# Weight requests of the opening chained two at a time, and one chunk's attention output transposed by DMA instead of TensorE, in a one-core transformer block

## The chip, the cores and the metric

One NeuronCore of a Trainium2 chip runs the whole kernel. The metric is device microseconds of one execution, without any host work; lower is better. Five engines work side by side and each takes its instructions in program order: TensorE (PE) multiplies and transposes, VectorE (DVE) and ScalarE (ACT) do elementwise work, GpSimd (POOL) and SyncE (SP) mostly issue DMA requests here.

## The reference

A block of 2048 tokens of width D = 576, in bfloat16, conditioned on one vector c:

```
mod = silu(c) @ w_mod                     # split in six rows: sa, ca, ga, sb, cb, gb
h = layernorm(x) * (1 + ca) + sa
x = x + ga * attention(h)                 # 32 heads of 18, wqkv and wo
h = layernorm(x) * (1 + cb) + sb
x = x + gb * (((h @ w_gate) * (h @ w_up)) @ w_down)      # inner width 4608
```

In the attention, token s looks at the eight tokens s, s-2, ..., s-14 (a window of 8, dilation 2); positions before the first token are masked. Weights are 576 x 1728 (wqkv), 576 x 576 (wo), 576 x 4608 (gate and up), 4608 x 576 (down) and 576 x 3456 (w_mod).

## The kernel before

**Stages.** The 2048 tokens are cut into eight chunks of CH = 256, each of two tiles of 128 ("halves" j = 0 and 1). The chunks are worked in five groups for the large matrix products: [0], [1, 2], [3, 4], [5, 6], [7]. Each group has a gate-and-up phase (`gate_up`, L968) and then a down phase (`down`, L1011; `down_last` for the last group). In both, a loop over 36 values of f goes through the inner width 128 columns at a time. Everything before the first gate phase is here called the opening: the modulation vectors, chunk 0 whole up to its second layernorm, and the first parts of chunks 1 and 2. The layernorms and attention of the later chunks run in pieces between the f steps of earlier groups.

**The order of work.** All five engines keep the order in which the program issues instructions. Between the f steps a planner (`timed`, L899, and `among` for the down phases) places pieces. A piece is a tuple of its cost on PE, its cost on DVE, the marks that it needs, the mark that it gives, a wait until that mark counts, and the call. The planner runs its own clock in these estimates; a thread (a list of pieces) goes on in order, and a piece is placed when its needs are met. The real dependencies are kept by semaphores; the numbers in a piece only move its place.

**Transfers.** SP issues, in program order on one queue, the input chunks (`load_x` L140 and `load_res` L144: tiles x_t and x_r), the gate and up weights and most transposes by DMA. A gate or up block covers FB = 4 values of f; `load_wgu` (L149) brings it by two requests of 512 KB (L158), one for gate and one for up, into a tile wgu. Three such tiles are in rotation (`wgup`), so blocks 0 to 2 of group 0 are loaded in the opening (L1213-1214); block 3 is put into the unused end of the tile hh (`wgu_home[3]`, last part of the program), blocks 4 and on are asked for as blocks come free. The 64 rows that 576 has beyond four times 128 come in two requests by `load_wgr` (L162), into wgr. The down weights are loaded by POOL (`load_wd`, L167, issued at L175; some into space named prod_t or hh). Ahead of the weight requests in the opening go the weights of the modulation (wmA, whose space is loaded a second time at L1211 under the name wmB; the records call it wmA both times) and, behind them, x_t and x_r of chunks 3, 1 and 4. `behind(dma, load)` adds a wait: the first request is not issued before the second has landed.

```
    load_wm_tail(wmB, 3, nc.sync)
    nc.sync.dma_start(wmB[:, 0:KF, :], w_mod[0:KF * P, 3 * D:5 * D]...)      # L1211
    load_wgr()
    for g in range(3):
        load_wgu(g)
```

**The attention output.** For a half, DVE multiplies the gathered values vsh by the attention weights (`b_mul`), adds them up (`b_add`) into o_sb (128 tokens x 640, of which the last 64 columns are a memset, L555, or a repetition, L558). The projection with wo needs o_sb transposed, in oT. This is done in one of two ways: `b_o` (L572) has PE transpose ten 128x128 squares (L578) into two PSUM tiles, which ACT copies to oT (L579, L580); `b_od` (L651) has SP issue one DMA transpose of 128x640 for a half (L653). `b_w(i, j)` (L655) then multiplies a half by wo on PE (L659 for the last 64 columns, L661 for the first 512), and DVE scales the result and adds the input, giving x1 of chunk i. The second layernorm follows (`b_ln`, `b_norm`), then a DMA transpose of its output into h2T (`b_td`, L693) and the modulation in place (`b_mod`). The DMA transpose of the first layernorm's output is `a_td` (L420).

Chunk 0 gets its output by another route; chunks 1 and 2 use `b_o`, chunks 3 to 7 `b_od` (`values_of`, L729; `out_of`).

**The first down phase** (group 0, two halves, four matmuls per f: L1021 into acc, L1026 into accr). Around it, chunk 1 ends its attention block (layernorm, h2T) and chunk 2 its values, output transpose, projection, layernorm and h2T; the list of chunk 2's pieces is `first_down` (L1390). In the same loop SP asks for blocks 0, 1 and 2 of group 1's gate weights behind f = 1, 20 and 26 (`asks`, L1038), and POOL for further down weights (`WD_ASKS`).

Of the kernel before, what the change touches and what calls it, by code (L numbers as in the profile page):

```python
# [18 lines left out]
P = 128  # L19
D = 576  # L20
DP = 640
KT = 5
KF = 4
# [13 lines left out]
FB = 4  # L37
# [5 lines left out]
PAIRED = (1, 3, 5, 7)  # L43
# [3 lines left out]
def kernel(  # L47
# [13 lines left out]
    nc = tc.nc  # L61
# [31 lines left out]
    def ps(shape, dt, name):  # L93
        return psp.tile(shape, dt, name=name, tag="bank")

    def js(j):
        return slice(j * P, (j + 1) * P)
# [14 lines left out]
    wgr = wts.tile([P, FF], BF, name="wgr")  # L112
# [34 lines left out]
    NG = len(GROUPS)  # L147
    NBLK = FT // FB

    def load_wgu(g):  # L150
        if g >= NG * NBLK:
            return
        cs = slice((g % NBLK) * NB, (g % NBLK + 1) * NB)
        wb = wgu_home.pop(g, None)
        if wb is None:
            wb = wgup.tile([P, KF, 2, NB], BF, name="wgu")
        for t, wsrc in enumerate((B_w_gate, B_w_up)):
            r = nc.sync.dma_start(wb[:, :, t, :], wsrc[0:KF * P, cs].rearrange("(k p) n -> p k n", p=P))  # L158
        wgu_blk[g] = wb
        wgu_in[g] = r  # L160

    def load_wgr():  # L162
        for t, wsrc in enumerate((B_w_gate, B_w_up)):
            r = nc.sync.dma_start(wgr[64 * t:64 * (t + 1), :], wsrc[KF * P:D, :])
        return r

    def load_wd(g):  # L167
# [49 lines left out]
    wmB = wmA  # L217
# [257 lines left out]
    def b_ld(i, j):  # L475
        b = bb.setdefault(i, dict(prod={}, vsh={}))
        base = HALO + i * CH + j * P - DIL * (W - 1)
        vsh = vshp.tile([P, W, DH, H], BF, name="vsh")
        vsrc = bass.AP(vd.tensor, vd.offset + base * D, [[D, P], [DIL * D, W], [1, D]])
        b["vsh"][j] = vsh  # L480
        r = nc.gpsimd.dma_start(vsh[:].rearrange("p w d h -> p w (d h)"), vsrc)  # L481
        b.setdefault("ld", r)
        return r
# [62 lines left out]
    def b_mul(i, j, w0, n=2):  # L546
        b = bb[i]
        v = b["vsh"][j][:, w0:w0 + n]
        at = b["attn"][:, j, w0:w0 + n, None, :].to_broadcast([P, n, DH, H])
        nc.vector.tensor_tensor(v, v, at, ALU.mult)  # L550
# [21 lines left out]
    def b_o(i):  # L572
        pA = ps([P, 4, CH], BF, "oT_pA")
        pB = ps([P, 1, CH], BF, "oT_pB")
        for m in range(KT):
            d = pA[:, m, :] if m < 4 else pB[:, 0, :]
            for j in range(ST):
                nc.tensor.transpose(d[:, js(j)], o_sb[:, j, m * P:(m + 1) * P], ident[:])  # L578
        nc.scalar.copy(oT[:, 0:4, :], pA[:])  # L579
        nc.scalar.copy(oT[:, 4, :], pB[:, 0, :])  # L580
# [70 lines left out]
    def b_od(i, tiles=range(ST)):  # L651
        for j in tiles:
            bb[i]["od"] = nc.sync.dma_start_transpose(out=oT[:, :, js(j)], in_=o_sb[:, j, :])  # L653

    def b_w(i, j):  # L655
        pw = ps([P, 512], F32, "pw")
        pwr = ps([P, 64], F32, "pwr")
        for m in range(KT):
            nc.tensor.matmul(pwr[:], lhsT=oT[:, m, js(j)], rhs=wo[:, m, 512:D], start=(m == 0), stop=(m == KT - 1))  # L659
        for m in range(KT):  # L660
            nc.tensor.matmul(pw[:], lhsT=oT[:, m, js(j)], rhs=wo[:, m, 0:512], start=(m == 0), stop=(m == KT - 1))  # L661
        xt = x1p.tile([P, D], BF, name="x1")
        nc.vector.tensor_tensor(xt[:, 512:D], pwr[:], ga_bc[:, 512:D], ALU.mult)
        nc.vector.tensor_tensor(xt[:, 0:512], pw[:], ga_bc[:, 0:512], ALU.mult)
        nc.vector.tensor_tensor(xt[:], xt[:], x_res[i][:, j, :], ALU.add)
        x1.setdefault(i, []).append(xt)
# [62 lines left out]
    def values_of(i, nxt=None):  # L729
        r = []  # L730
        for j in range(ST):
            r += [(0, 0.75, f"a{i}", "-", 0, lambda j=j, w=w: b_mul(i, j, w)) for w in range(0, W, 2)]
            r += [(0, 0.75, "", "-", 0, lambda j=j: b_add(i, j, 0)), (0, 0.75, "", "-", 0, lambda j=j: b_add(i, j, 1)),
                  (0, 1.2, "", f"o{i}{j}", 0, lambda j=j: b_add(i, j, 2))]
            if i in PAIRED[1:]:
                r.append((0, 0, "", f"O{i}" if j == ST - 1 else "-", 11.0 if i == 7 else 14.0, lambda j=j: b_od(i, (j,))))
            if nxt is not None:

                r.append((0, 0, f"v{nxt}", "-", 0, lambda j=j: behind(b_ld(nxt, j), bb[i]["od"]) if (i, j) == (3, 1) else b_ld(nxt, j)))
        return r  # L740
# [270 lines left out]
    def down(gi, hh, bg):  # L1011
        grp = GROUPS[gi]
        nj = ST * len(grp)
        last = FT - FB
        at, late = among(last, 0.25 * nj, bg)
        acc = [ps([P, 512], F32, "acc") for _ in range(nj)]
        accr = ps([P, 2 * ST, 64], F32, "accr")

        def mm_a(f, j):
            wb = wd_blk[gi * NBLK + f // FB]  # L1020
            nc.tensor.matmul(acc[j][:], lhsT=hh[:, f, js(j)], rhs=wb[:, f % FB, 0:512],  # L1021
                             start=(f == 0), stop=(f == FT - 1))

        def mm_r(f, j):
            wb = wd_blk[gi * NBLK + f // FB]
            nc.tensor.matmul(accr[:, j, :], lhsT=hh[:, f, js(j)], rhs=wb[:, f % FB, 512:D],  # L1026
                             start=(f == 0 and j == 0), stop=(f == FT - 1), skip_group_check=True)

        for f in range(last):
            for j in range(nj):  # L1030
                mm_a(f, j)
                mm_r(f, j)
            if f % FB == FB - 1:
                if gi in (1, 2) and f // FB == 1:
                    wd_home[gi * NBLK + 8] = value_space()[:, 0:FB * D].rearrange("p (k d) -> p k d", d=D)
                for k in WD_ASKS[gi].get(f // FB, ()):
                    load_wd(gi * NBLK + k)
            asks = (1, 5 * FB, 6 * FB + 2) if gi == 0 else (1, 4 * FB - 1, 6 * FB + 1)  # L1038
            if f in asks:
                load_wgu((gi + 1) * NBLK + asks.index(f))  # L1040
            for piece in at[f]:
                piece()
        xs = [t for i in grp for t in x1.pop(i)]
        for j in range(nj):
            for f in range(last, FT):
                mm_r(f, j)
        o_ts = [outp.tile([P, D], BF, name="o_t") for _ in range(nj)]
        t_r = outr.tile([P, 2 * ST, 64], BF, name="t_r")
        nc.vector.tensor_tensor(t_r[:, 0:nj, :], accr[:, 0:nj, :],  # L1049
                                gb_bc[:, None, 512:D].to_broadcast([P, nj, 64]), ALU.mult)  # L1050
        for j in range(nj):
            for f in range(last, FT):
                mm_a(f, j)
            nc.vector.tensor_tensor(o_ts[j][:, 0:512], acc[j][:], gb_bc[:, 0:512], ALU.mult)
        for j in range(nj):
            r0 = (grp[0] * ST + j) * P
            nc.vector.tensor_tensor(o_ts[j][:, 0:512], o_ts[j][:, 0:512], xs[j][:, 0:512], ALU.add)
            nc.vector.tensor_tensor(o_ts[j][:, 512:D], t_r[:, j, :], xs[j][:, 512:D], ALU.add)
            nc.sync.dma_start(out_flat[r0:r0 + P, :], o_ts[j][:])
        if gi in (0, 3):  # L1060
            load_wd(gi * NBLK + NBLK + 2)
        return late
# [58 lines left out]
    def behind(dma, load):  # L1121
        tc.add_manual_dep(dma.ins, load.ins.name, SYNC, reason="order of the loads")
# [81 lines left out]
    for dd4 in range(4):  # L1204
        nk = (DH - dd4 + 3) // 4
        wsrc = bass.AP(A_wo.tensor, A_wo.offset + dd4 * D, [[DH * D, H], [4 * D, nk], [1, D]])
# [1 line left out]
    load_x(2)  # L1208
    load_res(0)
    load_wm_tail(wmB, 3, nc.sync)  # L1210
    nc.sync.dma_start(wmB[:, 0:KF, :], w_mod[0:KF * P, 3 * D:5 * D].rearrange("(k p) n -> p k n", p=P))  # L1211
    load_wgr()
    for g in range(3):  # L1213
        load_wgu(g)
    cp, dv = nc.scalar.copy, nc.vector.tensor_copy
    x1c = x_in.pop(1)
    xn1, stat1, rsq1, norm1 = ln_parts(lambda j: x1c[:, j, :], "a", True)
# [170 lines left out]
           4: ([], [])}  # L1388

    def first_down(parts):  # L1390
        o2 = [(0, 0, "o21", "z2", 0.6, nop), (0.55, 0, "z2", "O2", 1.1, lambda: b_o(2)), (1.2, 1.35, "O2", "-", 0, lambda: b_w(2, 0)), (1.2, 1.35, "", "x2", 0.2, lambda: b_w(2, 1)),
              (0, 2.2, "", "s2", 0.7, lambda: b_ln(2)), (0, 1.5, "s2", "n2", 0.2, lambda: b_norm(2)), (0, 0, "n2", "T2", 6.0, lambda: b_td(2)),
              (0, 0, "T2", "M2", 0, lambda: (b_mod(2, (3, 4), False), b_mod(2, (0, 1, 2), True)))]
        return [[(0, 0, "", "-", 0, lambda: ld_prods(0))]] + parts[:-1] + [parts[-1] + o2]
# [16 lines left out]
    for gi, grp in enumerate(GROUPS):  # L1411
        hh_t = hhp.tile([P, FT * 2 * CH], BF, name="hh")
        n = CH * len(grp)
# [46 lines left out]
```

## Time and profile before

| | |
|---|---|
| median of three runs | 538.25 us (537.63 to 538.43) |
| the profiled execution | 538.37 us, of which the span from first to last instruction is 536.5 us |
| PE busy | 530.2 us, 99% of the span, 6365 matmuls and transposes |
| DVE, ACT, POOL busy | 319.3, 251.7 and 70.3 us |
| granted TensorE clock | 1.0 |
| moved by DMA | 114.81 MB, 214 GB/s in the mean |
| SP's queue (q1) | 67.25 MB in 84208 packets, 46.3% of 16 engines' span |
| POOL's queue (q0) | 46.40 MB in 11424 packets, 28.0% |
| 512 KB request of gate weights, issue to landing | median 5.7 us (of up weights 7.2) |

Times in the profile are microseconds from the start of the span, taken in one profiled execution. A line of the timeline gives the start, how long the run of equal instructions took, the engine, the source line and operation, the tiles written and read, shapes and how many. "SPq" and "POOLq" are the queues of these engines: such a line lasts from the first issue to the last of the group, not until the data has landed. In the list of DMA issues the last number is the median from issue to landing. The rows of forty digits show busy shares in tenths, forty equal slices of 13.4 us; PEclk is the granted clock in tenths. The chain of waits follows the work that ended last back to the start and shares the span out by engine.

### The profile page before, as it was taken

What the parts mean: (1) busy time and instruction counts of PE and PEld (TensorE: products, weight loads), DVE (VectorE), ACT (ScalarE), POOL (GpSimd) and SP (SyncE); (2) the same over time, 40 slices, a digit from 0 to 9 for tenths busy, and PEclk for the clock granted to TensorE, in tenths of its full rate; (3) what the DMA queues carried; (4) which work ended last, traced back from release to release, by engine and by line L of the source; (5) the groups of instructions that cost most, each with busy time, mean ns of one, the idle gap of its engine ahead of it and who ended that gap; (6) DMA issues with size and microseconds to landing.
All of it is one profiled execution on the core that took longest, in us unless ns stands there. A gap on an engine that the chain in (4) does not pass through costs nothing.

```text
span 536.5 us, 14991 instructions
## 1 busy us (share of the span) xinstructions
PE 530.2 (99%) x6365; PEld 327.8 (61%) x6365; DVE 319.3 (60%) x748; ACT 251.7 (47%) x629; POOL 70.3 (13%) x109
## 2 busy tenths in 40 slices
PE   8999999999999999999999999999999999999997
PEld 4787888758875444555544454555544454558875
DVE  5898888869777785508467797513527733032212
ACT  4866887605666544103655543104556541006630
POOL 8104013202000110111000011110010101110210
PEclk9999999999999999999999999999999999999999
DMA  9999999899987854969354944963395594659741
GB/s 287 304 272 365 317 267 333 282 256 242 273 203 186 275 107 123 281 184 304 94 170 119 317 125 137 268 185 109 104 320 154 154 301 107 208 140 291 238 124 35
DMA packets 96004, 114.81 MB, mean 214 GB/s; under 512 B 29217, under 2 KB 84722, under 8 KB 95810
## 3 DMA queue, kind: packets, MB, share of 16 engines
q1 hardware_dynamic: 84208, 67.25, 46.3%
q0 software_dynamic: 11424, 46.40, 28.0%
q8 instruction: 50, 0.82, 0.6%
q10 hardware_dynamic: 306, 0.21, 0.1%
q14 instruction: 16, 0.13, 0.1%
HBM read 103.07 MB, written 4.74 MB: 201 GB/s over the span
## 4 chain that ended last, share of the span: by engine, by line
PE 97%; DMA 1%; DVE 0%; SPq 0%; issue 0%; ACT 0%
PE pg L774 29%; PE pu L774 24%; PE acc L1021 20%; PE pq L774 4%; PE pq L442 3%; PE accr L1026 3%; PE acc L1076 3%; PE pv L774 2%; PE pw L774 2%; PE lgT L501 2%; PE pv L465 1%; PE pw L661 1%; DMA wmA<-in_w_mod_dram 1%; PE po L616 1%; PE pwj L638 0%; PE accr L1079 0%
## 5 line engine op out<-in xcount | busy, mean ns | idle before, releaser
L774 PE MATMUL pg<-h2T,wgu 64*128 64x512 bf16 (+1 forms) x1400 | 267.7, 328 | 0.3 <-issue 0.3
L774 PE MATMUL pu<-h2T,wgu 64*128 64x512 bf16 (+1 forms) x1400 | 266.1, 328 | 0.0
L774 PEld LDWEIGHTS <-wgu 64*128 64x128 bf16 x2800 | 140.0, 94 | 90.8 <-issue 0.9
L825 ACT CAST u_sb<-pu 128x512 bf16<-128x512 f32 (+1 forms) x169 | 83.9, 496 | 155.9 <-PE pg L774 150.9
L828 DVE TENSOR_TENSOR hh<-g_sb,u_sb 128x512 bf16<-128x512 bf16 x133 | 56.3, 423 | 109.4 <-ACT g_sb L826 108.5
L1021 PE MATMUL acc<-wd,hh 128*128 128x512 bf16 x344 | 85.7, 380 | 0.0
L1021 PEld LDWEIGHTS <-hh 128*128 128x128 bf16 x504 | 49.0, 98 | 59.7 <-issue 1.5
L826 ACT CAST g_sb<-pg 128x512 bf16<-128x512 f32 (+1 forms) x169 | 84.9, 502 | 0.0
L1026 PE MATMUL accr<-wd,hh 128*128 128x64 bf16 x344 | 62.4, 193 | 0.0
L774 PE MATMUL pu<-h2T,wgr 64*128 64x256 bf16 (+1 forms) x191 | 61.9, 324 | 0.0
L774 PE MATMUL pg<-h2T,wgr 64*128 64x256 bf16 (+1 forms) x191 | 61.9, 324 | 0.0
L1026 PEld LDWEIGHTS <-hh 128*128 128x128 bf16 x504 | 45.8, 98 | 1.2
L175 POOL DMA_DIRECT2D wd<-in_B_w_down_dram x29 | 21.8, 753 | 183.5 <-PE accr L1026 148.2
L550 DVE TENSOR_TENSOR vsh<-vsh,attn 128x1152 bf16<-128x1152 bf16 x56 | 39.5, 750 | 0.0
L489 DVE TENSOR_TENSOR prod_t<-qT,kT 128x1280 bf16<-128x1280 bf16 x36 | 28.2, 819 | 3.5 <-ACT kT L845 2.7
L774 PEld LDWEIGHTS <-wgr 64*128 64x128 bf16 x382 | 19.7, 94 | 15.0 <-issue 2.3
L1021 PE MATMUL acc<-prod_t,hh 128*128 128x512 bf16 x112 | 28.1, 380 | 0.0
L774 PE MATMUL pq<-hT,wqk 64*128 64x256 bf16 (+1 forms) x450 | 26.8, 258 | 0.0
L774 PEld LDWEIGHTS <-wqk 64*128 64x128 bf16 x450 | 21.3, 94 | 5.3
L1049 DVE TENSOR_TENSOR t_r<-accr,gb_bc 128x256 bf16<-128x256 f32 (+1 forms) x4 | 1.5, 378 | 38.2 <-PE accr L1026 38.2
L481 POOL DMA_DIRECT2D vsh<-vd x14 | 12.6, 901 | 86.6 <-DVE o_sb L558 61.8
L1026 PE MATMUL accr<-prod_t,hh 128*128 128x64 bf16 x112 | 21.6, 193 | 0.0
(224 smaller groups left out, 630.4 us busy)
## 6 DMA issues: line engine op xcount, KB each, us to landing
wgu<-in_B_w_gate_dram SPq DMA_DIRECT2D x41, 512.0 KB, 5.7
wgu<-in_B_w_up_dram SPq DMA_DIRECT2D x41, 512.0 KB, 7.2
wd<-in_B_w_down_dram POOLq DMA_DIRECT2D x29, 576.0 KB, 4.9
vsh<-vd POOLq DMA_DIRECT2D x14, 1152.0 KB, 8.5
prod_t<-in_B_w_down_dram POOLq DMA_DIRECT2D x8, 576.0 KB, 6.5
hh<-in_B_w_down_dram POOLq DMA_DIRECT2D x6, 576.0 KB, 6.9
x_t<-in_A_x_dram SPq DMA_DIRECT2D x8, 288.0 KB, 6.0
x_r<-in_A_x_dram SPq DMA_DIRECT2D x8, 288.0 KB, 7.7
```

The source lines that it names most:

```text
L175: return nc.gpsimd.dma_start(wb[:], B_w_down[r0:r0 + FB * P, :].rearrange("(k p) n -> p k n", p=P))
L442: nc.tensor.matmul(pq[:, gi, :], lhsT=wqk[:, kt, m * P:(m + 1) * P], rhs=hT[:, kt, cols], start=(kt == order[0] and not (by_k and gi)), st ...
L481: r = nc.gpsimd.dma_start(vsh[:].rearrange("p w d h -> p w (d h)"), vsrc)
L489: nc.vector.tensor_tensor(prod, aa[i]["qT"][:], aa[i]["kT"][:, :, off:off + CH], ALU.mult)
L550: nc.vector.tensor_tensor(v, v, at, ALU.mult)
L774: return nc.tensor.matmul(out, lhsT=lhs, rhs=rhs, start=first, stop=last, skip_group_check=True)
L825: nc.scalar.copy(u[:, c, :], pu)
L826: nc.scalar.copy(g[:, c, :], pg)
L828: return lambda: nc.vector.tensor_tensor(hh[:, f - c:f + 1, :], g, u, ALU.mult)
L1021: nc.tensor.matmul(acc[j][:], lhsT=hh[:, f, js(j)], rhs=wb[:, f % FB, 0:512], start=(f == 0), stop=(f == FT - 1))
L1026: nc.tensor.matmul(accr[:, j, :], lhsT=hh[:, f, js(j)], rhs=wb[:, f % FB, 512:D], start=(f == 0 and j == 0), stop=(f == FT - 1), skip_grou ...
L1076: nc.tensor.matmul(acc[i][:], lhsT=hh[:, f, js(j)], rhs=wb(f)[:, c0:c1], start=(f == 0), stop=(f == FT - 1))
```

## The change

**The opening.** From the long load of wmB on, seven more requests are noted in a list `longs`: the two of `load_wgr` and gate and up of blocks 0, 1 and 2. With wmB's that makes nine, and each but the first two waits, by `behind`, until the one two places before it has landed; the second wgr request is the first to wait (for wmB), and the gate request of block 0 waits for the first wgr request. After block 2 the list is cleared: later requests do not wait in this way. They stand behind these on SP's queue, though.

**Chunk 2's output.** `b_o(2)` is dropped. `values_of(2)` issues a DMA transpose of a half (`b_od`) as soon as the half is added up, giving the mark D0 or D1, which counts for the planner 8 us later; `b_w(2, 0)` needs D0 and `b_w(2, 1)` D1, separately.

**The asks.** Blocks 1 and 2 of group 1's gate weights are asked for behind f = 26 and 27 of the first down phase, not 20 and 26.

```diff
+    longs = []
+
+    def in_turn(r):
+
+        if longs:
+            longs.append(r)
+            if len(longs) > 2:
+                behind(r, longs[-1 - 2])
+        return r
+
     def load_wgu(g):
...
-            r = nc.sync.dma_start(wb[:, :, t, :], wsrc[0:KF * P, cs].rearrange("(k p) n -> p k n", p=P))
+            r = in_turn(nc.sync.dma_start(wb[:, :, t, :], wsrc[0:KF * P, cs].rearrange("(k p) n -> p k n", p=P)))
...
     def load_wgr():
         for t, wsrc in enumerate((B_w_gate, B_w_up)):
-            r = nc.sync.dma_start(wgr[64 * t:64 * (t + 1), :], wsrc[KF * P:D, :])
+            r = in_turn(nc.sync.dma_start(wgr[64 * t:64 * (t + 1), :], wsrc[KF * P:D, :]))
         return r
...
-            if i in PAIRED[1:]:
+            if i == 2:
+                r.append((0, 0, "", f"D{j}", (8, 8)[j], lambda j=j: b_od(i, (j,))))
+            elif i in PAIRED[1:]:
                 r.append((0, 0, "", f"O{i}" if j == ST - 1 else "-", 11.0 if i == 7 else 14.0, lambda j=j: b_od(i, (j,))))
...
-            asks = (1, 5 * FB, 6 * FB + 2) if gi == 0 else (1, 4 * FB - 1, 6 * FB + 1)
+            asks = (1, 26, 27) if gi == 0 else (1, 4 * FB - 1, 6 * FB + 1)
...
-    nc.sync.dma_start(wmB[:, 0:KF, :], w_mod[0:KF * P, 3 * D:5 * D].rearrange("(k p) n -> p k n", p=P))
+    longs.append(nc.sync.dma_start(wmB[:, 0:KF, :], w_mod[0:KF * P, 3 * D:5 * D].rearrange("(k p) n -> p k n", p=P)))
     load_wgr()
     for g in range(3):
         load_wgu(g)
+    longs.clear()
...
-        o2 = [(0, 0, "o21", "z2", 0.6, nop), (0.55, 0, "z2", "O2", 1.1, lambda: b_o(2)), (1.2, 1.35, "O2", "-", 0, lambda: b_w(2, 0)), (1.2, 1.35, "", "x2", 0.2, lambda: b_w(2, 1)),
+        o2 = [(1.2, 1.35, "D0", "-", 0, lambda: b_w(2, 0)), (1.2, 1.35, "D1", "x2", 0.2, lambda: b_w(2, 1)),
```

## The prediction, made before the result was seen

> **What bounds the kernel now.** I read the page first: busy shares, granted clock, chain.
>
> ```profile
> PE 530.2 (99%) x6365; PEld 327.8 (61%) x6365; DVE 319.3 (60%) x748; ACT 251.7 (47%) x629; POOL 70.3 (13%) x109
> ...
> PEclk9999999999999999999999999999999999999999
> DMA  9999999899987854969354944963395594659741
> ...
> PE 97%; DMA 1%; DVE 0%; SPq 0%; issue 0%; ACT 0%
> ```
>
> PE is busy 99% of the span of 536.5 us at an undiminished clock and is 97% of the chain, so an instruction taken off PE shortens the run by what it occupies there, and a wait added on PE lengthens it in full: no idle time further on can absorb it. Removing waits can bring little, since PE idles only 536.5 - 530.2 = 6.3 us, most of it at the two ends. The DMA row matters too: up to about 107 us (the first eight slices of 13.4 us) the transfer engines are as full as PE, so a transfer delayed there cannot catch up.
>
> Then the timelines of the two places edited. PE in the first down phase, with the transposes that go:
>
> ```profile
> 113.74 0.38 PE L1021 MATMUL acc<-prod_t,hh 128*128 128x512 bf16 x1
> 113.96 0.19 PE L1026 MATMUL accr<-prod_t,hh 128*128 128x64 bf16 x1
> 113.99 0.61 PE L578 MATMUL oT_pA<-shifts,o_sb 128*128 128x128 bf16 x8
> 114.44 0.28 PE L578 MATMUL oT_pB<-shifts,o_sb 128*128 128x128 bf16 x2
> 114.55 0.38 PE L1021 MATMUL acc<-prod_t,hh 128*128 128x512 bf16 x1
> ```
>
> SP's queue in the opening, and for the last weight request its line in the list of issues, whose last number is microseconds to landing:
>
> ```profile
> 22.90 4.89 SPq L158 DMA_DIRECT2D wgu<-in_B_w_gate_dram  x1
> 27.84 3.48 SPq L158 DMA_DIRECT2D wgu<-in_B_w_up_dram  x1
> 31.36 3.58 SPq L158 DMA_DIRECT2D wgu<-in_B_w_gate_dram  x1
> 34.98 1.69 SPq L158 DMA_DIRECT2D wgu<-in_B_w_up_dram  x1
> ...
> 40.73 1.39 SPq L158 DMA_DIRECT2D hh<-in_B_w_up_dram  x1
> ```
> ```profile
> hh<-in_B_w_up_dram SPq DMA_DIRECT2D x1, 512.0 KB, 18.0
> ```
>
> Block 3 of the first gate phase (it lies in hh) is thus complete at 40.73 + 18.0 = 58.7; PE first reads it at 62.07. Last, SP and DVE in the first down phase, where the new transfers go in:
>
> ```profile
> 104.68 2.55 SPq L693 DMA_TRANSPOSE h2T<-xn  x2
> 107.29 0.57 SPq L158 DMA_DIRECT2D wgu<-in_B_w_gate_dram  x1
> ```
> ```profile
> 106.79 0.09 DVE L555 MEMSET o_sb<- 128x32 uint32 x1
> ...
> 112.10 0.09 DVE L555 MEMSET o_sb<- 128x32 uint32 x1
> ```
>
> The memsets end the two halves of chunk 2's attention output: ready at 106.88 and 112.19.
>
> **Part 1, what leaves PE and ACT.** Ten 128x128 transposes go. The matmul ahead of them hands over at 113.99 and the next starts at 114.55: **-0.56 us** on PE. ACT loses the two evictions (L579 1.01 us, L580 0.38 us); it had idled 8.9 us before them, so nothing follows.
>
> **Part 2, the new wait on PE.** In the built order the projection of half 0 (L659, L661) moves from behind f = 27 to behind f = 20; that of half 1 stays behind f = 29. One f takes 0.49 us (50 pairs of matmuls from 101.73 to 113.99), so PE asks for half 0 at 101.73 + 21 x 0.49 = 112.0, that is 5.1 us after the data is ready. Half 1 is asked for where L659 now runs second, 118.22, less 0.56: 117.66, that is 5.5 us after its data. SP stands idle before both and issues at once. How long does a 128x640 transpose take? Rows of the same stage of other groups, with weight loads from POOL in flight: 3.3 (213.07), 4.3 (332.44), 4.4 (449.57), 5.4 (450.87), 5.5 (126.07); in this very stage 6.1 and 9.8 (104.68, 105.98); alone 2.6 (201.24). The bounds are therefore 2.6 and 9.8. I take 4.4, the row nearest in its surroundings (a POOL load issued 0.8 us earlier, as here at 106.12): half 0 lands at 111.4, in time by 0.6; half 1, by 5.4, at 117.7, just in time. **0 us**, with ends 0 and 106.95 + 9.8 - 112.0 = 4.7. What is queued behind a late projection is every later matmul.
>
> Moved with it: two of chunk 2's products (1.4 us) go ahead of chunk 1's layernorm statistics on DVE, and SP now issues half 0, then chunk 1's two h2T transposes (from 104.68 to about 108.2, 1.2 us each), then waits for half 1 at 112.19, and only then asks for weight blocks 1 and 2 of the next gate phase (107.29 to about 113.5). With the 9.8 row h2T lands at 119.2; DVE needs 1.37 us to modulate it and PE reads it from 122.5 - 0.56: covered by 1.4. Block 1 landed 12.8 us after its second issue (107.91): 114.1 + 12.8 = 126.9, against its first use at about 128.4 (four f of 1 us and two value pairs of 1 us after 122.5): covered by 1.5; block 2 (15.9) by 1.7. Cost 0.
>
> **Part 3, the opening.** Seven requests now wait for the one two before them: the second remainder load wgr, and gate and up of blocks 0 to 2. Before, SP simply pushed; the rows of 4.89, 3.48 and 3.58 us show it held back by a full queue, and the landings follow each other every 1.5 us (21.29 + 15.3 = 36.6, 22.21 + 15.9 = 38.1). So 512 KB are 1.5 us of transfer. A 512 KB request into a quiet queue lands after
>
> ```profile
> wgu<-in_B_w_gate_dram SPq DMA_DIRECT2D x1, 512.0 KB, 4.0
> ```
>
> (412.29). With two in flight, two requests move in 4.0 + 0.05 us instead of 3.0: a hole of 1.05 us per pair, the engines idle. Walking it through from the landings that the edit leaves alone (wmB, called wmA in the records, 28.85, first wgr 31.57, second wgr about 35.1): the six weight requests issue at 31.7, 35.2, 36.7, 39.3, 40.8, 43.4 with three holes, 3 x 1.05 = 3.15 us. POOL has little to fill them with before 44 (0.1 MB at 34), so everything behind on SP's queue comes 3.15 us later as long as the engines stay full, which the DMA share of 1.02 to 1.1 between 31 and 63 says they do:
> - block 3: 58.7 + 3.15 = 61.9, against 62.07: just in time.
> - block 4: gate landed at 53.51 + 9.0 = 62.5, up by the 1.5 us spacing at 64.0 (its own landing is not recorded): 67.1, against PE's first use at 66.00: **1.1 us late, paid on PE**.
> - chunk 3's input: issued some 7 us later (43.8), landing about 52 instead of 45.4; DVE wants it at 51.83, and its idle 0.29 and 1.53 us before 58.90 and 61.59 take that up. 0.
> - block 5 lands at 66.8 + 3.15 = 70.0, against 70 + 1.1. 0.
>
> Bounds: nothing, if the hardware's own hold-back already had only about two requests under way; and with 5.0 per request (the up load of the same quiet pair) (5.0 + 0.05 - 3.0) x 3 = 6.2 us, so 6.2 - 2.0 = 4.2 us at block 4. The value of 4.0 is the nearer: it is one request's own duration, the 5.0 includes queueing behind its partner.
>
> The Trainium skill, DMA: Bandwidth & Descriptors, section on the anatomy of one DMA, prices a request at 2.0 us fixed plus its bytes at 436 GB/s. That would be 3.2 us for 512 KB and, as an estimate from that page, 0.25 us per hole and no late block at all; it gives the case without a stall below. This trace does not agree: 4.0 us, and 1.5 us between landings.
>
> **Sum**: -0.56 + 0 + 1.1 = +0.55. The profiled run took 538.37 (span 536.5 and 1.9 around it), 0.1 over the median of 538.25; added to the median: **538.8 us**.
>
> **The rivals.**
> - **No stall at all**: holes add to less than 2.0 us in sum (or the holds change nothing, since SP was held back anyway: the 4.89 us row speaks for it, the 4.0 us row against). 538.25 - 0.56 = 537.7.
> - **The transpose is late on PE**, slower: price is its time to landing less 5.1 us. With 6.1 it is 1.0; from 6.7 on the kernel is slower by over 0.2%, with the 9.8 row +4.1: 542.4. For it: both rows of this very stage are above 6; against it: in the new order half 0 goes first and the weight loads of SP come after.
> - **The opening's holes are larger**, slower: at 5.0 per request +3.7, 541.9. For it: POOL's loads from 44 on take the larger part (0.87 MB against 0.20 MB of SP's queue between 46 and 49), so a request pushed behind 44 moves slowly.
> - **PE gains more than the records show**, faster: if its transposes also cost it the 1.39 us of evictions, 536.3. Against it: PE ran matmuls without a gap straight behind them. The Trainium skill, TensorE: Matmul & The Clock Gate, Part 4 on transposes, has about 275 ns for one in a kernel, which would be 2.75 us for ten, an estimate from that page; the trace has ten in 0.56 us and does not agree.
>
> **How the numbers follow.** Forecast 0.38, of which 0.08 ends above the bound; no stall 0.30; late transpose 0.14; larger holes 0.14; more than the records 0.04. A measurement of this kernel can tell about 0.2% (1.1 us) from no change. Slower by more: 0.08 + 0.14 + 0.14 = 0.36; faster by more: 0.04; within: 0.60. The range begins at 537.3, the case without a stall less 0.4 for the spread of the runs (537.63 to 538.43), and ends at 541.3, which takes in both slow rivals up to about 3.6 us of stall and leaves out their far ends.
>
> **What would show it.** After: no L578 at 114, L659 twice with oT landing by DMA; PE idle before the first of them is the late transpose, by its length. PE idle at 62 (hh) or 66 (wgu) is the opening; the landings of block 3 and 4 should be near 61.9 and 67.1. Landings of the six requests 4 us after issue and a lower DMA rate between 33 and 44 show the holes; an unchanged rate there refutes them and makes 537.7 the result. PE idle in any other place would prove the accounting wrong.

## The result and the profile after

The changed kernel takes 549.94 us (548.60 to 550.72, four runs) against 538.05 (537.63 to 538.43, four runs) for the kernel before on the same chip: a ratio of 1.0222, with a 95% interval of 1.0206 to 1.0238. The forecast was 538.8 with a range up to 541.3. The profiled execution took 550.72, that is 12.35 more than the profiled one of before. One execution of a later run, the one with three requests under way, had a granted clock of 0.56 from end to end (929.20 us) and is in none of the times below. The lines that answer to those shown of before:

```profile
PE 531.5 (97%) x6327; PEld 325.7 (59%) x6355; DVE 319.5 (58%) x748; ACT 251.1 (46%) x627; POOL 70.1 (13%) x109
...
PEclk9999789999999999999999999999999999999999
DMA  9989997979895676697733973994285693758731
...
PE 88%; DMA 6%; DVE 4%; ACT 1%; issue 1%; SPq 0%
```

PE is busy for about as long as before, but its share of the chain has fallen from 97% to 88%. DMA and DVE have taken it. The granted clock, 9 in all forty slices before, falls to 7 and 8 in the fifth and sixth slice (55 to 82 us). So the loss has a place. PE's timeline there (the brackets give the idle time ahead of a line and what ended it):

```profile
56.37 0.27 PE L786 MATMUL pg<-h2T,wgu 64*128 64x256 bf16 x1
59.84 0.28 PE L786 MATMUL pu<-h2T,wgu 64*128 64x256 bf16 x1 [3.19 <-DMA wgu<-in_B_w_up_dram]
...
60.61 0.27 PE L786 MATMUL pg<-h2T,wgr 64*128 64x256 bf16 x1
66.99 0.39 PE L786 MATMUL pu<-h2T,wgr 64*128 64x256 bf16 x1 [6.11 <-DVE dd L540]
```

First PE waits 3.19 us for the up weights of block 2. Then it waits 6.11 us for a PSUM bank that DVE has yet to read (dd, in chunk 1's softmax). DVE's timeline says why it is late (the first line is of before, the others are of the changed kernel):

```profile
51.83 0.81 DVE L283 BATCH_NORM_STATS2 ln_statsa<-x_t 128x6 f32<-128x288 bf16 x2
```
```profile
51.08 0.43 DVE L840 TENSOR_TENSOR hh<-g_sb,u_sb 128x512 bf16<-128x512 bf16 x1 [0.33 <-issue]
61.06 0.82 DVE L293 BATCH_NORM_STATS2 ln_statsa<-x_t 128x6 f32<-128x288 bf16 x2 [9.55 <-DMA x_t<-in_A_x_dram]
...
66.24 0.69 DVE L540 TENSOR_TENSOR dd<-lg,mx 128x512 f32<-128x512 bf16 x1
```

DVE keeps program order, and the first statistics of chunk 3 stand ahead of the softmax. It waits 9.55 us for chunk 3's input. SP's queue around these two requests, and their lines in the list of issues (then the input's line of before, where it was pushed at 36.77):

```profile
41.70 0.37 SPq L168 DMA_DIRECT2D wgu<-in_B_w_gate_dram  x1
43.07 0.37 SPq L168 DMA_DIRECT2D wgu<-in_B_w_up_dram  x1
43.49 1.39 SPq L140 DMA_DIRECT2D x_t<-in_A_x_dram  x1
```
```profile
wgu<-in_B_w_up_dram SPq DMA_DIRECT2D x1, 512.0 KB, 16.7
x_t<-in_A_x_dram SPq DMA_DIRECT2D x1, 288.0 KB, 17.5
```
```profile
x_t<-in_A_x_dram SPq DMA_DIRECT2D x1, 288.0 KB, 8.6
```

Block 2's up lands at 59.8. The input, pushed at 43.49 where the prediction had 43.8, lands at 61.0 and not at 52 (before: 45.4). The clock, by stretches (PE busy first, PEclk third from the end):

```profile
60.00:64.00 4.00, 0.88 (x16) 0.54 (x12) 2.80 (x10) 0.62 (x3) 0.00 (x0) 0.68 1.09 357
64.00:67.00 3.00, 0.01 (x2) 0.01 (x2) 2.96 (x6) 2.53 (x8) 0.00 (x0) 0.50 1.10 348
67.00:71.00 4.00, 4.00 (x38) 2.89 (x40) 1.74 (x3) 2.08 (x5) 0.00 (x0) 0.50 1.44 279
71.00:72.00 1.00, 1.00 (x16) 0.76 (x12) 0.47 (x2) 0.82 (x3) 0.00 (x0) 0.66 0.23 59
```

While PE stands in the second wait, its clock is halved, and it stays so for over 4 us of work after: 4 x 0.5 + 0.34 = 2.3 us lost. The last wait is that for half 0 of chunk 2's output:

```profile
124.70 0.32 PE L669 MATMUL pwr<-wo,oT 128*128 128x64 bf16 x5 [1.18 <-DMA oT<-o_sb]
```

The sum is 3.19 + 6.11 + 2.3 + 1.18 - 0.56 = 12.2, against 12.35 measured.

### The profile page after: what moved, and what is told of

Read it like the earlier page. It is cut to its first block, busy times and chain, and to the rows that moved or that the text cites. A ratio compares the mean times of both kernels' runs of the same rounds, so it can differ in the third digit from the quotient of the medians.

```text
span 549.0 us, 14950 instructions
## 1 busy us (share of the span) xinstructions
PE 531.5 (97%) x6327; PEld 325.7 (59%) x6355; DVE 319.5 (58%) x748; ACT 251.1 (46%) x627; POOL 70.1 (13%) x109
## 3 DMA queue, kind: packets, MB, share of 16 engines
q1 hardware_dynamic: 85552, 67.57, 45.4%
## 4 chain that ended last, share of the span: by engine, by line
PE 88%; DMA 6%; DVE 4%; ACT 1%; issue 1%; SPq 0%
PE pg L786 27%; PE pu L786 22%; PE acc L1033 18%; PE pq L786 3%; DMA x_t<-in_A_x_dram 3%; PE accr L1038 3%; PE acc L1088 3%; PE pv L786 2%; PE pq L452 2%; PE pw L786 1%; DMA wgu<-in_B_w_up_dram 1%; PE lgT L511 1%; PE pw L671 1%; DMA oT<-o_sb 1%; PE busy L213 1%; PE po L626 1%
## 5 line engine op out<-in xcount | busy, mean ns | idle before, releaser
L786 PEld LDWEIGHTS <-wgu 64*128 64x128 bf16 x2800 | 138.5, 95 | 97.6 <-DMA wgu<-in_B_w_up_dram 4.1
L1033 PE MATMUL acc<-wd,hh 128*128 128x512 bf16 x328 | 83.7, 380 | 0.1
```

The costliest lines, as they stand in the source:

```text
L786: return nc.tensor.matmul(out, lhsT=lhs, rhs=rhs, start=first, stop=last, skip_group_check=True)
```

## The experiments

A kernel with the chain alone is called "opening only" here, one with the DMA transposes and the new asks alone "output only". (The chain notes eight requests beside wmB's, two of `load_wgr` and six of blocks 0 to 2, not seven as the section on the change says; seven of the nine wait.) "Before" is the median on the same chip in the same batch: 537.68 in the first, 537.98 in the second, 537.92 in the third.

### Each part alone

Opening only: `o2`, `values_of` and `asks` as before.

> The kernel before with the opening's chain alone (no DMA transpose for chunk 2, the old asks). Theory (collision: the chained requests are pushed after POOL has started its two 1152 KB gathers at 41 and 44 us, and from then on a request of SP takes 13 to 17 us): PE stalls as in the changed kernel, about 3.4 us at 56 (block 2) and 6.3 at 61 (DVE stands behind chunk 3's input), then some 5 us at a halved clock; only the 1.3 us wait at 123 goes and the 0.56 us of transposes come back: 549.2. Rival of the prediction (holes between the requests, everything later by 3 to 4 us and no more): 541 to 542. Rival (the output part matters most): below 540.

Measured: 546.46 (546.31 to 550.84), ratio 1.0177 (1.0136 to 1.0219), +8.8 us. PE has one wait, the second of the two:

```profile
64.46 0.39 PE L784 MATMUL pu<-h2T,wgr 64*128 64x256 bf16 x1 [7.11 <-DVE dd L540]
```

The input landed 15.3 us after its push. Block 2's up landed at 55.5 here, just in time, and the input at 58.6 instead of 61.0, which is why this lies below the 549.2 expected. The rest is as in the changed kernel: 7.11 and about 2.2 us of halved clock behind it (64.5 to 69).

Output only: the wait is not made.

```diff
-                behind(r, longs[-1 - 2])
+                pass
```

> The kernel before with chunk 2's DMA transposes and the new asks alone, the opening as it was. Theory: 0.56 us of PE transposes go and PE waits 1.3 us for half 0, whose transpose takes 6.1 to 6.3 us: 538.05 - 0.56 + 1.3 = 538.8. The forecast's own step (half 0 in time): 537.5. Rival (the two parts disturb each other, and this one carries some of the 12 us): 540 and more.

Measured: 540.96 (539.77 to 543.90), ratio 1.0062 (1.0038 to 1.0086), +3.3. The profiled execution, 543.90, is the longest:

```profile
115.82 0.45 PE L669 MATMUL pwr<-wo,oT 128*128 128x64 bf16 x5 [4.17 <-DMA oT<-o_sb]
```

Half 0's transpose took 8.8 us; the clock was 0.50 from 116 to 121, some 2.5 us. Expected were 1.3 us of waiting, and 4.2 were met here: the time lies in the rival's range (540 and more), but the trace shows the theory's own wait, only longer. The medians of the two parts add up, 8.8 + 3.3 = 12.1 against 11.9 for both, but not term by term, so this is partly chance: in the changed kernel the trace has 3.19 + 6.11 + 2.3 = 11.6 us in the opening and 1.18 - 0.56 = 0.6 in the output. What is to be explained is mostly the opening.

### POOL's gathers held back, and the input ahead

The first theory was a collision. POOL's two gathers (vsh, 1152 KB each) begin at 41 and 44 us, and a request of SP pushed after that is slow. Two edits of opening only:

```diff
-    b_ld(1, 0)
+    behind(b_ld(1, 0), wgu_in[2])
```

> The opening's chain alone, and POOL's first gather (vsh of chunk 1, not used before 74 us) waits until block 2's up weights have landed. Collision theory: block 2's up lands by about 47 us, chunk 3's input by about 50, DVE no longer stands at 51.5, no stall of PE above 1 us: 538 to 539.5. Holes theory (the 1.3 MB not moved between 30 and 44 us are what is missing, whoever moves first): the stalls stay at 3 to 4 us in sum, 541 to 542. Volume theory (the gathers only collide later, with block 3 and 4): 542 to 546.

Measured: 544.81 (541.52 to 549.32), ratio 1.0136 (1.0068 to 1.0204). SP's requests are quicker now (the input 6.7 us, landing at 50.9; block 2's up landed at 50.2, where 47 was expected), and DVE does not stand. But now POOL's own load of the last modulation weights lands at 66.1 (59.2 before), and PE waits for that:

```profile
66.21 0.67 PE L390 MATMUL pa<-hh,sc_bc 128*32 128x144 bf16 x16 [5.08 <-DMA hh<-in_w_mod_dram]
```

The collision theory had 538 to 539.5. It was right on the input and on DVE and wrong on the end. Part of this new wait is not a matter of bytes: the load stands behind the held gather in POOL's program order, and so it was pushed at 54.27 in place of 50.02. Behind the wait the clock was at half until 69.4, which cost some 1.6 us.

```diff
     for g in range(3):
+        if g == 2:
+            load_x(3)
         load_wgu(g)
```
(and no `load_x(3)` further down)

> The opening's chain alone, with chunk 3's input requested ahead of block 2 instead of behind it. Collision theory: the input is pushed at about 39, lands by 46 to 48, so DVE does not stand, the 6.3 us stall and the halved clock behind it (2.1 to 2.4 us) go, and block 2's wait of 3.4 us stays or grows to 5: 541.5 to 543.5. Rival (PE's second stall is weights that are late in any case, not DVE's queue): 547 and more.

Measured: 542.83 (540.84 to 544.34), ratio 1.0088 (1.0057 to 1.0119). The time is in the range expected, and DVE does not stand, so that wait was indeed the input. But three shorter waits for weights take its place, for block 2 and then for block 3 (in hh):

```profile
58.32 0.28 PE L784 MATMUL pu<-h2T,wgu 64*128 64x256 bf16 x1 [1.64 <-DMA wgu<-in_B_w_up_dram]
```
```profile
64.21 0.28 PE L784 MATMUL pg<-h2T,hh 64*128 64x256 bf16 x1 [0.71 <-DMA hh<-in_B_w_gate_dram]
65.73 0.28 PE L784 MATMUL pu<-h2T,hh 64*128 64x256 bf16 x1 [1.24 <-DMA hh<-in_B_w_up_dram]
```

The expectation had a wait of 3.4 to 5 us for block 2 alone and a clock that stays up. Here the clock fell all the same (0.50 from 67 to 69, some 1.7 us in all), and PE waited 1.16 us more at 88.55, for ACT, so that the number came out by a sum that was not the expected one.

### The collision without the chain

The clean test: the kernel before, and only the input's request (with what stands behind it) is pushed late.

```diff
-    load_x(3)
+    behind(load_x(3), wgu_in[2])
```
(`load_x` returns its request)

> The kernel before, no chain; only the request of chunk 3's input (and what stands behind it on SP's queue) waits until block 2's up weights have landed (44.7 us in the trace of before). Nothing is held back before that, so no bytes go unmoved up to 44. Collision theory: the input is pushed after POOL's first gather (41 us), takes 15 to 17 us and lands near 60; DVE stands from 52, PE 5 to 8 us, then a lowered clock for 1 to 2: 543 to 547. Holes theory (only the unmoved bytes cost): no more than 538.7.

Measured: 538.35 (537.09 to 541.52), ratio 1.0008 (0.9992 to 1.0024): no loss. The collision theory, with 543 to 547, is refuted. The input was pushed at 43.18, within 0.1 us of opening only (43.25), and the first gather began at 41.1 (40.8 there), yet:

```profile
x_t<-in_A_x_dram SPq DMA_DIRECT2D x1, 288.0 KB, 5.3
```

5.3 us here, 15.3 there. What differs is what lies ahead of it on SP's queue. Here block 2 has landed; there the gate and up of block 2, 1024 KB pushed within the last two microseconds, are still to be moved (SP's queue moved 0.04 MB from 41.58 to 43.25). The time of the push does not matter, the unmoved bytes ahead do.

The expectation had said that no bytes go unmoved up to 44. They did; this is SP's queue from 30 to 44, where before moved 4.00 MB:

```profile
q1 hardware_dynamic: 3076, 3.11, 77.2%
```

The 0.89 MB less were bytes of the input and of block 3 themselves, which nothing waited for yet: the input landed at 48.5, DVE took it at 51.55; block 3's up landed at 61.4 (before 58.7), and PE first read that block at 61.80. So unmoved bytes cost nothing as long as the transfer that owes them lands ahead of its reader.

### The bytes

The same two stretches by queue (packets, MB, share), first from 30 to 44 us for before and then for the changed kernel:

```profile
q1 hardware_dynamic: 3865, 4.00, 99.4%
q0 software_dynamic: 118, 0.27, 7.7%
```
```profile
q1 hardware_dynamic: 2183, 2.53, 72.0%
q0 software_dynamic: 118, 0.47, 11.1%
```

and from 44 to 57 for the changed kernel, with the line for all queues:

```profile
DMA packets 2087, 4.46 MB, mean 343 GB/s; under 512 B 131, under 2 KB 1414, under 8 KB 2086
q0 software_dynamic: 765, 3.10, 65.9%
q1 hardware_dynamic: 1321, 1.35, 33.0%
```

The chain leaves 4.00 - 2.53 = 1.47 MB of SP's queue (q1) unmoved by 44. From about 45 on the engines are full, at 343 GB/s over both queues, but SP's queue gets only 1.35 MB in 13 us of that, 0.104 MB a us; POOL's (q0) gets 0.24. At SP's mean rate 1.47 MB are 14 us, and the input landed 61.0 - 45.4 = 15.6 us later than before. In opening only: (4.00 - 2.49) MB at 1.58 / 13 = 0.12 MB a us are 12.4 us, and 13.1 were measured. This is the debt theory; it was tried on a third order and on the number of requests under way.

With both gathers moved behind POOL's loads for which PE waits:

```diff
-    b_ld(1, 0)
-    b_ld(1, 1)
...
-lambda: (load_wm5(), load_wd(0))
+lambda: (load_wm5(), load_wd(0), b_ld(1, 0), b_ld(1, 1))
```

> The opening's chain alone, with both of POOL's gathers of chunk 1 (first used at 74 us) moved behind the loads of the last modulation weights and of down block 0, so that they go out at about 50. The bytes unmoved between 30 and 44 stay unmoved. If they cost only through what stands last in line for something that PE or DVE waits for: SP's requests land 5 to 9 us after their push, the modulation weights by 58, no stall above 1 us, 537.7 to 539.5. Holes theory (a debt of 1.2 MB, 3.5 to 4 us, whatever the order): 541 to 542. Volume theory (the gathers then delay block 4, block 5 and chunk 3's transposes): 540 to 545.

Measured: 544.74 (542.40 to 549.54), ratio 1.0139 (1.0095 to 1.0183). Block 2, the input, block 3 and the modulation weights are all in time in the profile (542.40, the shortest run). Block 4 is late:

```profile
66.34 0.28 PE L784 MATMUL pg<-h2T,wgu 64*128 64x256 bf16 x1 [0.54 <-DMA wgu<-in_B_w_gate_dram]
68.45 0.39 PE L784 MATMUL pu<-h2T,wgu 64*128 64x256 bf16 x1 [1.83 <-DMA wgu<-in_B_w_up_dram]
```

None of the three orders tried got rid of the debt; it moved from input to modulation weights to blocks 2 and 3 to block 4. (By 57 both queues together had moved 9.09 MB since 30 before, 7.74 in opening only, and 7.14, 7.66 and 7.49 in the three orders.)

With three requests under way, and with one:

```diff
-            if len(longs) > 2:
-                behind(r, longs[-1 - 2])
+            if len(longs) > 3:
+                behind(r, longs[-1 - 3])
```
(and `> 1`, `longs[-1 - 1]`)

> The opening's chain alone, with three requests under way instead of two. Debt theory (what counts is how many bytes of SP's queue are unmoved at 44 us, when POOL's gathers begin to take the larger part, since they are then repaid at SP's own 0.11 MB a us and not at the engines' 0.34): three under way close the holes, SP's queue moves 3.5 to 4.0 MB between 30 and 44 (before 4.00, with two 2.49), chunk 3's input lands by 49, 537.7 to 539.5. Rival (the wait itself costs, its semaphore and SP standing still): at least half of the 8.8 us stays, 542 to 547.

Measured: 539.00 (537.41 to 543.09, nine runs), ratio 1.0027 (1.0004 to 1.0050), +1.1. The trace is of one more execution of the same kernel:

> The same kernel as with three requests under way, for an undisturbed profile. Debt theory: SP's queue moves 3.5 to 4.0 MB between 30 and 44 us, block 2's up and chunk 3's input are served before the gathers take over, the input lands by 49, DVE does not stand at 51, PE has no wait above 1 us in the opening or one of 1 to 3 for block 4: 538 to 541. Rival (the semaphore wait itself costs): SP's queue stays near 2.5 MB.

Measured: 538.11, beside 537.73 for before, one execution of each. Between 40 and 80 us PE has no wait above 0.51 us. SP's queue from 30 to 44, and the input:

```profile
q1 hardware_dynamic: 3413, 3.50, 87.7%
```
```profile
x_t<-in_A_x_dram SPq DMA_DIRECT2D x1, 288.0 KB, 6.2
```

> The opening's chain alone, with one request under way. Debt theory: each of eight requests takes 3.7 to 4 us by itself, SP's queue moves about 1.7 to 1.9 MB between 30 and 44, block 2 and chunk 3's input come 8 to 15 us later than with two, and PE waits for weights first: 553 to 565. Rival (a fixed price of the chain, not of the bytes): 545 to 550.

Measured: 559.62 (557.84 to 560.59), ratio 1.0397 (1.0374 to 1.0419), +21.7; SP's queue from 30 to 44:

```profile
q1 hardware_dynamic: 642, 1.28, 37.7%
```

With 4.00, 3.50, 2.49 and 1.28 MB moved, the chain alone costs 0, 1.1, 8.8 and 21.7 us. A fixed price of the wait is refuted: the same kind of wait with three costs 1.1. What the debt theory says of two under way holds, with limits:

- With one under way the time is in the range expected, but not by the share: SP's queue moved less than the 1.7 to 1.9 MB expected, the engines moved only 126 GB/s from 57 to 66, and the input was pushed at 64.42 and landed 5.4 us later. There the chain itself is the delay.
- The bytes of SP's queue at 44 are no price list: 2.68 to 2.94 MB cost 5.2 to 7.1 us in the three orders, and 3.11 MB cost nothing in the kernel without the chain. The order decides whose reader waits.
- SP's rate is a mean. Before, SP's queue moved 0.02 MB in all from 53 to 56, and in the kernel without the chain 0.89 MB less at 44 brought block 3's up only 2.7 us later.

### The output part

Half 0's projection 7 f later:

```diff
-                r.append((0, 0, "", f"D{j}", (8, 8)[j], lambda j=j: b_od(i, (j,))))
+                r.append((0, 0, "", f"D{j}", (11.5, 8)[j], lambda j=j: b_od(i, (j,))))
```

> The output part alone, with half 0's mark counted 11.5 instead of 8 us after its transpose, which puts its projection 7 f (3.4 us) later. Theory (the loss of the output part is PE's wait for half 0, 4.3 us in the trace with the output part alone): the wait falls to 0 to 0.9 and the 0.56 us of transposes are gained, 537.1 to 538.2. Rival (the loss lies in the later requests of weight blocks 1 and 2, or elsewhere): 540 and more.

Measured: 538.12 (537.55 to 539.03), ratio 1.0005 (0.9996 to 1.0013). The whole loss of the output part is gone, so it was PE's wait. Half 0's transpose took 7.0 us here, with POOL's loads as before, and PE came later.

POOL's load that stood beside the transpose, held:

```diff
-                    load_wd(gi * NBLK + k)
+                    r = load_wd(gi * NBLK + k)
+                    if (gi, k) == (0, 9):
+                        behind(r, bb[2]["od"])
```

> The output part alone; POOL's load of down block 9 (used in the next down phase only) waits for the last transpose of chunk 2's output issued so far. Contention theory: half 0's transpose took 8.8 us because two loads of 576 KB were under way; with one it takes 6.5 or less, PE waits up to 2 us: 537.7 to 539.3. Rival (the transposes are slow by themselves, three on one queue): unchanged, 540.5 to 541.5.

Measured: 538.58 (537.32 to 539.77), ratio 1.0008 (0.9996 to 1.0021). Half 0's transpose took 5.2 us in place of 8.8, and PE's wait shrank to this:

```profile
112.19 0.32 PE L669 MATMUL pwr<-wo,oT 128*128 128x64 bf16 x5 [0.52 <-DMA oT<-o_sb]
```

So it is mostly the POOL load that slows the transpose: with the load beside it 6.3, 7.0 and 8.8 us were seen (changed kernel, projection later, output only), without it 5.2, and 4.9 in the next run. Both edits together:

> The output part alone, with both remedies: half 0's projection 7 f later and POOL's load of down block 9 held behind the transposes. No wait of PE at 111 to 118 is left, so only the 0.56 us of transposes are gained: 537.4 to 537.6 against a kernel before of 538.0, at the edge of what can be told. Rival (a gain on PE does not reach the end, as it did not with the later projection alone): 538.0 to 538.5.

Measured: 538.13 (537.74 to 539.33), ratio 1.0005 (0.9995 to 1.0014). The gain of 0.56 us is there in its stage. From the first matmul of the down phase to the first of the next gate phase it is 122.49 - 101.73 = 20.76 us before, and 122.65 - 102.45 = 20.20 here. In the whole time it is not seen, as the rival had it, and why is open. The start of the stage varies more than that: 101.19 with the later projection alone, 102.45 here. No version beat the kernel before.

## Why the prediction was wrong

- **PE is the bound, an added wait is paid in full**: right, and too little. A wait of over 4 us also cost 1.6 to 3.0 us of halved clock (2.3 in the changed kernel). The sum and both slow rivals priced a wait at its length alone.
- **-0.56 for the transposes**: right in the stage (20.76 to 20.20). The fourth rival's 2.75 us took ten times the duration of one; the trace records each as 0.22 us, but they overlap and follow each other every 0.056.
- **Half 0 in time, by 4.4 us**: wrong. It took 6.3 (8.8 in output only). The rival's price, landing less 5.1, gives 1.2, and 1.18 was measured; in output only it gives 3.7, and 4.17. Both rows of this very stage, 6.1 and 9.8, had been the better ones; the row taken came from another group. The same instruction (L653) had taken 5.6 to 7.9 us four times in later stages of the kernel before, which the prediction did not list.
- **Half 1, h2T, blocks 1 and 2 of the next group in time**: right. Half 1 took 5.1, the h2T transposes 7.8 and 7.0, and PE and DVE show no wait of over 0.9 us for them in the changed kernel.
- **Holes of 3.15 us**: right in size. Over both queues 4.31 - 3.02 = 1.29 MB were not moved from 30 to 44; at 343 GB/s that is 3.8 us.
- **"so everything behind on SP's queue comes 3.15 us later as long as the engines stay full"**: this step failed; it is the step that made the forecast wrong. Full engines do not serve SP's queue at their own rate. The bytes in arrears are repaid at what POOL's gathers leave, 0.104 MB a us in place of 0.343, and so 3.8 us became some 14 (the input came 15.6 later). The third rival had quoted the row (0.87 MB against 0.20 between 46 and 49) and then priced the holes by 5.0 us for each request, +3.7, and not by the share.
- **Chunk 3's input landing at 52, cost 0**: this follows from it: 61.0, 6.11 us on PE and 2.3 of halved clock. Block 2's up weights had no line in the sum at all; they cost 3.19.
- **Block 4, 1.1 us**: not seen; PE stood before it came to that block. The prediction had named the sign: PE idle anywhere but at 62 (hh), at 66 (wgu) or ahead of half 0 would prove the accounting wrong. It idled from 56 and from 61, for block 2 and for DVE.

Two rules of the Trainium skill stand behind rows here. DMA: Bandwidth & Descriptors, section on queues, rings and completion order, has each transfer engine go round its queues packet by packet. The trace agrees in direction: from 44 to 57 SP's queue had more packets (1321 to 765), each of about 1 KB against POOL's 4 KB, and fewer bytes. No run here changed the size of packets. TensorE: Matmul & The Clock Gate, Part 1, has the clock halved after about 3.4 us of idling and restored after about as long at work. The traces agree on the first in part: 3.19 us left the clock at 1.0 and 4.17 halved it, but it fell 2.5 us after PE had stopped in output only, 4.8 with the gather held back, and 0.6 us into the second wait of the changed kernel. For the second they show 3.2 to 6.0 us. In each trace here the low clock behind a wait lasted 3.4, 6.8 or 10.2 us.

## What to carry to other kernels

Where two queues share full transfer engines, estimate a delay on one of them as its unmoved bytes divided by that queue's own rate in the stretch where they are repaid, not by the engines' rate, and count it only where it makes a transfer later than its reader; look for what another queue starts next. List each transfer behind the edit with its first reader, and ask what stands in program order behind that reader on its engine. Price a wait of PE of over some 4 us with some 2 us more for the clock (1.6 to 3.0 here).

## What the runs showed that was not expected

- Two 512 KB requests under way do not fill the engines here (222 GB/s from 30 to 44 in opening only), three nearly do (271), and SP's queue pushed freely, before, does (308).
- The push time of a request told nothing: 43.2 us gave 5.3 us in one kernel and 15.3 in the other, by the 1024 KB ahead of it.
- A transpose of 128x640 by DMA took from 2.6 us (half 1 with the load held) to 8.8 us; with one POOL load of 576 KB less beside it half 0 took 5.2 and 4.9 in place of 6.3 to 8.8.
- The halved clock also followed two short waits close together, 0.54 and 1.83 us with one matmul between (0.59 from 68 to 70 us in the run with the gathers last), though neither alone is as long as the 3.19 us that left it at 1.0. In the run with the input ahead it followed 0.71 and 1.24 us in the same way (0.50 from 67 to 69).
